# Attention feeding a wide two-layer network on one core: another order list for the first 14 steps

## The chip, the cores and the metric

The kernel runs on one core of one Trainium2 chip. Its time is the device time of one execution in microseconds (us). Five engines work side by side, each through its own instruction queue in order: PE (TensorE, matmuls and transposes), ACT (ScalarE, exponentials, logarithms, copies), DVE (VectorE, reductions and elementwise work), POOL (GpSimd, elementwise work and some transfers) and SP (SyncE, which issues nearly all transfers). An instruction starts when it is at the head of its queue and the results and buffers that it needs are there.

## The reference

```python
# attention: B, H, S, D = 4, 8, 768, 64, block 32, window 16
k_sum = k.reshape(B, H, nb, block, D).max(axis=3)
v_sum = v.reshape(B, H, nb, block, D).mean(axis=3)
scores_l = scale * q @ k.T         # kept where |i - j| < window, else -1e9
scores_s = scale * einsum('bhsd,bhnd->bhsn', q, k_sum) + log(block)
a = softmax(concat([scores_l, scores_s]))     # sum + 1e-9 below
x = (a @ concat([v, v_sum])).transpose(0, 2, 1, 3).reshape(B * S, H * D)
# network: x 3072x512, w_in 512x2048, w_out 2048x512, weights in float64
h = x @ w_in
g = (a[0] + a[1]*h + a[2]*h**2 + a[3]*h**3) / (1 + abs(b[0])*abs(h) + abs(b[1])*h**2 + 1e-6)
out = g @ w_out
```

## The kernel before

The 3072 rows of x are worked in 6 groups of 512, and the 2048 hidden columns in 16 chunks of 128, so that there are 96 steps of one group and one chunk. A step has three parts. The first layer makes h (128x512, in one of two PSUM buffers) with 12 matmuls. The rational function ("gelu" in the code) takes 5 DVE operations and a final one on POOL, with squares, logarithm and exponential on ACT; it writes gh and gl, a high and a low part. The second layer adds 12 matmuls into four accumulators po (po0 to po3). Each factor is split into a high and a low part (xh and xl, gh and gl, two halves of a weight) and three of the four products are summed, which is why a step has 24 matmuls of 512 columns.

The weights come as float64, 1 MB a chunk. They are decoded on the chip: after the load (wr), a scaling on ACT, a byte step on POOL, a shift-and-or on DVE (`SCALAR_TENSOR_TENSOR wr<-wr`), a rounding to the high part (CAST on ACT, or a POOL transfer) and the low part on DVE. The first group needs all 16 chunks decoded.

Attention is made in 48 "halves" of 64 queries (all 8 heads). A half goes through scores (sc, PE), the masked score and its row minimum (4 DVE reductions), exponentials (4 on ACT, then the row sum sm), reciprocal and scaling, transposes (pt, PE), their copy (pts), the product with the values (av, PE), and the parts xh (a cast on ACT or DVE) and xl (a subtraction on DVE). Halves 0 to 7 make the first group's x. The value means that every half of the first batch needs come from window averages on PE (tile vf), copied by ACT into the last 24 rows of vw0 and vw1: before these copies no av matmul can start. The first h matmul needs xh of all 8 halves.

Two PSUM pools matter below: ps_h has two buffers, shared by h, the early pt and the spare matmuls; ps_a has two for the later sc, av and a few squares. So h of step n waits until the buffer of the tile two places earlier in ps_h is free, which for h is when DVE's second-to-last use of it is over (`tu<-tu,cs,h`).

What sets the order in the first 14 steps (NSTRICT = 14) is the table TEXT (line 48), a list of 583 tokens that a loop hands to `token()` one by one; the class Kept records that the instructions of an engine stay in the order in which they were handed out. A token issues the next stage of one thing: `h3` the next stage of half 3, `w4` the next step of decoding chunk 4, `W4` its load, `x5` the next third of the first layer of step 5, `ga5` to `gk5` parts of its rational function, `y5` the next quarter of its second layer, `v2` one term of the value averages, `V2` the load of a window of values, `K`/`k` a load and block maximum of keys, and `Z0` to `Z5` a spare matmul (128x312) whose result is not used. Since each engine has its own queue, a token moved past tokens of other engines alone changes nothing. After the list, the rest of the steps is scheduled by priorities that the change does not touch.

Of the kernel before, what the change touches and what calls it, by code (L numbers as in the profile page):

```python
# [44 lines left out]
LAG = 3  # L45
SOFF = 12
NWARM = 6
TEXT = ("h10 Q0 S0 K0 k0 K2 k2 K1 k1 K3 B9 k3 h8 B8 h2 h3 M0 N0 h3 h3 h3 W0 w0 h2 V2 Q1 h0 h1 h1 h2 N1 h2 V1 h3 h3 V4 V0 W1 W3 Z0 v2 Z4 h0 h0 w0 w0 h4 h2 h1 h1 h1 h4 h0 h0 v4 h2 w0 F0 "
# [11 lines left out]
AVGH = 40  # L60
NCONST = NK + P + AVGH + NB
NREST = (S - HPG * HQ) // P
# [23 lines left out]
def tile_kernel(ctx, tc, qfirst, qw_in, kraw, kwin, vpad, vred, wio, a, b, cboth, out):  # L86
# [660 lines left out]
    strict |= {pe, dve, act, gps, syn}  # L747
    for what in TEXT.split():
        token(what.rstrip("0123456789"), int(what.lstrip("abcdefghijklmnopqrstuvwxyzABCDEFGHIJKLMNOPQRSTUVWXYZ")))
# [100 lines left out]
```

## Time and profile before

| what | value |
|---|---|
| time, median of 3 runs | 629.33 us (628.99 to 630.05) |
| the profiled execution, its own time | 629.38 us |
| its span (first to last instruction) | 627.6 us |
| PE busy | 616.0 us (98%) |
| DVE busy | 563.1 us (90%) |
| ACT busy | 455.4 us (73%) |
| POOL busy | 262.5 us (42%) |
| mean granted clock of PE | 0.996 of full speed |

Busy time of an engine is a mean over stages with different limits: the profile of the first 165 us differs from the rest, so that a row that names a stretch tells more than the whole. A time in brackets behind an instruction, as `[1.78 <-ACT vw L114]`, is how long its engine was idle before it and what ended the wait. All compute instructions carry the line L114 (the helper of Kept), so tiles are told by their names.

### The profile page before, as it was taken

The page shows a single profiled execution, that of the slowest core. Times are in us where ns is not written, and L with a number is a line of the kernel's source. Part 1 is how long each engine was busy: PE and PEld are TensorE (multiplying, and loading weights), DVE is VectorE, ACT ScalarE, POOL GpSimd, SP SyncE. Part 2 cuts the span into 40 slices and gives each one's busy share as a digit, 9 for nine tenths or more (in the row PEclk, how much of TensorE's full clock was granted, in tenths as well). Part 3 has the DMA queues.
Part 4 walks back from the last instruction along what each step waited for, and adds up shares of the span by engine and source line. Part 5 has one row for each costly group of instructions (what it writes and reads, how often), then busy time and mean ns, then how long its engine had stood idle before and what let it go on. Part 6 is the DMA issues. An engine that isn't in the chain of part 4 may idle for free.

```text
span 627.6 us, 11968 instructions
## 1 busy us (share of the span) xinstructions
PE 616.0 (98%) x4126; PEld 491.4 (78%) x4126; DVE 563.1 (90%) x1148; ACT 455.4 (73%) x1022; POOL 262.5 (42%) x359
## 2 busy tenths in 40 slices
PE   8789999999999999999999999999999999999997
PEld 4376777778788888888888888888888888888885
DVE  6989999999798999799999999888888988889885
ACT  3979998986966766867767867757767765755563
POOL 2768747735433435323433245334143242132221
PEclk9989999999999999999999999999999999999999
DMA  8989869332443453333433524224233120100001
GB/s 337 390 296 315 250 178 280 126 116 68 151 131 126 119 159 122 135 99 125 125 106 123 162 83 130 71 66 134 87 113 122 38 66 1 67 1 0 2 1 67
DMA packets 50836, 79.80 MB, mean 127 GB/s; under 512 B 6248, under 2 KB 32040, under 8 KB 48856
## 3 DMA queue, kind: packets, MB, share of 16 engines
q1 hardware_dynamic: 49064, 74.52, 35.7%
q0 software_dynamic: 1280, 4.39, 3.1%
q8 instruction: 32, 0.52, 0.4%
q14 instruction: 28, 0.23, 0.1%
q10 hardware_dynamic: 432, 0.13, 0.1%
HBM read 59.83 MB, written 14.75 MB: 119 GB/s over the span
## 4 chain that ended last, share of the span: by engine, by line
PE 84%; ACT 6%; DVE 4%; POOL 2%; issue 2%; DMA 1%; DVEq 0%; ACTq 0%; POOLq 0%
PE po L114 39%; PE h L114 37%; PE av L114 3%; ACT ss L114 3%; PE sc L114 3%; PE pt L114 1%; DVE tu L114 1%; POOL ss L114 1%; DVE tq L114 1%; DMA cs<-in_b_dram 1%; ACT wearly L114 1%; POOL gl L114 1%; ACT ta L114 1%; DVE gh L114 1%; ACT wr L114 1%
## 5 line engine op out<-in xcount | busy, mean ns | idle before, releaser
L114 POOL TENSOR_TENSOR gl<-tu,ta 128x512 fp32r<-128x512 f32 x96 | 131.2, 1366 | 281.7 <-DVE tu L114 153.7
L114 ACT ACTIVATE ta<-tq,cs 128x512 f32<-128x512 f32 x96 | 69.6, 725 | 72.9 <-DVE tq L114 72.1
L114 PE MATMUL po<-wearly,gh 128*128 128x512 f32 x384 | 120.2, 394 | 0.0
L114 PE MATMUL po<-w,gh 128*128 128x512 f32 x384 | 119.9, 394 | 0.0
L114 POOL TENSOR_SCALAR ss<-ss,sm 128x120 f32<-128x120 f32 x176 | 85.3, 505 | 40.4 <-DVE sm L114 39.6
L114 PE MATMUL h<-xh,wearly 128*128 128x512 f32 x384 | 96.9, 391 | 0.1
L114 PE MATMUL h<-xh,w 128*128 128x512 f32 x384 | 96.5, 390 | 0.0
L114 PEld LDWEIGHTS h<-xh,wearly 128*128 128x128 f32 x384 | 71.5, 188 | 16.4 <-PE spare L114 1.1
L114 PEld LDWEIGHTS po<-wearly,gh 128*128 128x128 f32 x384 | 70.8, 188 | 16.6 <-issue 1.8
L114 PEld LDWEIGHTS h<-xh,w 128*128 128x128 f32 x384 | 71.8, 188 | 15.0
L114 PEld LDWEIGHTS po<-w,gh 128*128 128x128 f32 x384 | 71.1, 188 | 15.7 <-issue 1.3
L114 DVE SCALAR_TENSOR_TENSOR gh<-tu,cs,ta 128x512 fp32r<-128x512 f32 x96 | 74.6, 777 | 8.3 <-ACT ta L114 1.5
L114 ACT ACTIVATE ss<-ss,sm 128x120 f32<-128x120 f32 x188 | 71.8, 386 | 12.7 <-DVE sm L114 12.6
L114 PE MATMUL po<-wearly,gl 128*128 128x512 f32 x192 | 75.1, 391 | 0.3 <-POOL gl L114 0.2
L114 ACT ACTIVATE tu<-h,cs 128x512 f32<-128x512 f32 x96 | 74.8, 779 | 0.4 <-PE h L114 0.4
L114 PE MATMUL po<-w,gl 128*128 128x512 f32 x192 | 74.9, 390 | 0.0
L114 DVE SCALAR_TENSOR_TENSOR tu<-tu,cs,tq 128x512 f32<-128x512 f32 x96 | 72.3, 753 | 2.9
L114 DVE SCALAR_TENSOR_TENSOR tu<-tu,cs,h 128x512 f32<-128x512 f32 x96 | 71.3, 743 | 2.8
L114 DVE SCALAR_TENSOR_TENSOR tq<-tq,gh 128x512 f32<-128x512 f32 x96 | 67.4, 703 | 2.8
L114 ACT ACTIVATE ta<-h,cs 128x512 f32<-128x512 f32 x95 | 64.7, 681 | 3.5 <-POOL gl L114 3.5
L114 DVE TENSOR_TENSOR tu<-tu,h 128x512 f32<-128x512 f32 x96 | 64.9, 676 | 0.0
L114 ACT ACTIVATE ta<-ta 128x512 f32<-128x512 f32 x96 | 60.8, 633 | 2.5
(97 smaller groups left out, 903.3 us busy)
## 6 DMA issues: line engine op xcount, KB each, us to landing
wr<-in_wio_dram SPq DMA_DIRECT2D x15, 1024.0 KB
cross<-tb SPq DMA_DIRECT2D x32, 256.0 KB, 2.0
vw<-in_vpad_dram SPq DMA_DIRECT2D x40, 192.0 KB, 3.4
kw<-in_kwin_dram SPq DMA_DIRECT2D x36, 192.0 KB, 3.3
pts<-cross SPq DMA_DIRECT2D x96, 64.0 KB, 1.9
out_dram<-o SPq DMA_DIRECT2D x23, 256.0 KB, 2.0
qw<-in_qw_dram SPq DMA_DIRECT2D x40, 128.0 KB, 2.6
kr<-in_kraw_dram SPq DMA_DIRECT2D x12, 384.0 KB, 4.5
```

Source lines behind the costliest of these rows:

```text
L114: out = getattr(self.engine, name)(*args, **kw)
```

## The change

Only TEXT changes. It has the same 583 tokens in another order; nothing else in the file differs, so every engine executes the same work. The first two rows of the list of before and of after:

```diff
-TEXT = ("h10 Q0 S0 K0 k0 K2 k2 K1 k1 K3 B9 k3 h8 B8 h2 h3 M0 N0 h3 h3 h3 W0 w0 h2 V2 Q1 h0 h1 h1 h2 N1 h2 V1 h3 h3 V4 V0 W1 W3 Z0 v2 Z4 h0 h0 w0 w0 h4 h2 h1 h1 h1 h4 h0 h0 v4 h2 w0 F0 "
-        "w0 w0 h3 h3 h4 h4 h4 h1 w1 h2 h2 h6 h7 h7 h7 h7 V5 h0 h0 h0 h5 V6 v1 v0 h6 h7 h6 h5 w1 w1 h4 v8 V3 w3 w3 h5 v9 h5 h5 h7 V7 w3 v5 w1 w1 v6 h5 I0 i0 h6 w3 w3 A8 v3 w3 v7 m0 h0 "
...
+TEXT = ("K2 K0 Q0 k0 S0 h10 h11 k2 K1 k1 K3 k3 M0 h8 h2 h2 h0 W0 Z1 h3 h3 Z4 Q1 h6 h1 h1 V0 N0 h2 h2 h2 h2 N1 V1 V2 h3 h3 B8 w0 B9 w0 h0 h0 h0 h3 h3 Z3 h1 h1 h3 h7 h7 h7 w0 h9 v2 W1 "
+        "h0 h4 h3 v1 h5 h7 h1 h6 h0 V4 v4 h4 w1 w1 h6 w1 h0 W3 h0 v0 h1 V7 w0 w0 h5 h5 h4 h4 h7 w1 w1 V6 Z5 v7 w1 w3 w3 w3 v6 V3 v3 h4 h4 h7 F0 v8 v9 V5 v5 h5 h5 I0 i0 w3 A9 A8 h2 w3 "
...
```

The loads of chunks 1 and 3 (tokens `W1`, `W3`) stood together at places 38 and 39 of the list; they stand at 57 and 75 now. In SP's queue, which is all that a load's place among the tokens decides, the 13th and 14th transfers were those of W1 and W3; now the 12th is W1 and the 14th W3, with one window of values between them, and two key loads stand ahead of the first queries.

On ACT the exponentials of the halves are taken in another order. The rows around the copies of the value means (vw0, vw1) were these; ss6 and sm6 are the exponentials and the sum of half 6, wr the scaling of a chunk, pts5 the copied transposes of half 5:

```order
L114 ACTIVATE ss6_418,sm6_419<-ss6_418,sm6_419 128x120 x4
L114 ACTIVATE sm6_419<-sm6_419 128x4
L114 CAST wearly_103<-wr3_259 128x1024
L114 COPY vw0_101<-vf_263 24x512
L114 COPY vw1_102<-vf_263 24x512
L114 CAST xh0_478<-av0_480 128x4x64
L114 ACTIVATE wr4_530<-wr4_530 128x1024
L114 COPY pts5_565<-pt5_551 120x512
L114 ACTIVATE wr2_538<-wr2_538 128x1024
L114 CAST xh0_478<-av4_574 128x4x64
L114 CAST xh0_478<-av3_586 128x4x64
L114 ACTIVATE ss8_524,sm8_525<-ss8_524,sm8_525 128x120 x4
```

and now they are these:

```order
L114 ACTIVATE ss5_412,sm5_413<-ss5_412,sm5_413 128x120 x4
L114 ACTIVATE sm5_413<-sm5_413 128x4
L114 CAST wearly_103<-wr3_400 128x1024
L114 COPY vw0_101<-vf_324 24x512
L114 COPY vw1_102<-vf_324 24x512
L114 CAST xh0_475<-av0_477 128x4x64
L114 ACTIVATE ss6_374,sm6_375<-ss6_374,sm6_375 128x120 x4
L114 ACTIVATE sm6_375<-sm6_375 128x4
L114 ACTIVATE wr2_494<-wr2_494 128x1024
L114 COPY pts5_543<-pt5_530 120x512
L114 CAST xh0_475<-av3_552 128x4x64
L114 ACTIVATE ss8_537,sm8_538<-ss8_537,sm8_538 128x120 x4
```

The exponentials of half 6 stood ahead of the two copies and stand behind the first xh now; those of half 8 come behind the second xh and those of half 9, not in these rows, still ahead of the last xh.

On PE the first steps of the network stood as follows; h0_1 is h of group 0, step 1, vf1 the averages of the second batch, po0_0 the first accumulator of group 0 and spare3 the token Z3:

```order
L114 MATMUL spare3_728<-both_95 128x312
L114 MATMUL h0_1_730<-xh0_478,wearly_103 128x512 x4
L114 MATMUL h0_1_730<-xl0_479,wearly_103 128x512 x4
L114 MATMUL h0_1_730<-xh0_478,wearly_103 128x512 x4
L114 MATMUL vf1_759<-vf1_0_755,both_95 32x128 x4
L114 MATMUL h0_2_796<-xh0_478,wearly_103 128x512 x4
L114 MATMUL h0_2_796<-xl0_479,wearly_103 128x512 x4
L114 MATMUL h0_2_796<-xh0_478,wearly_103 128x512 x4
L114 MATMUL vf1_759<-vf1_1_757,both_95 32x128 x4
L114 MATMUL po0_0_828<-wearly_103,gh0_0_688 128x512 x2
```

and now, from the same h0_1 on:

```order
L114 MATMUL h0_1_747<-xh0_475,wearly_103 128x512 x4
L114 MATMUL pt9_755<-both_95,ss9_546 120x128 x4
L114 MATMUL h0_1_747<-xl0_476,wearly_103 128x512 x4
L114 MATMUL h0_1_747<-xh0_475,wearly_103 128x512 x4
L114 MATMUL h0_2_787<-xh0_475,wearly_103 128x512 x4
L114 MATMUL h0_2_787<-xl0_476,wearly_103 128x512 x4
L114 MATMUL h0_2_787<-xh0_475,wearly_103 128x512 x4
L114 MATMUL pt8_811<-both_95 128x312
L114 MATMUL pt8_811<-both_95,ss8_537 120x128 x4
L114 MATMUL vf1_819<-vf1_0_734,both_95 32x128 x12
L114 MATMUL vf1_819<-vf1_1_736,both_95 32x128 x4
L114 MATMUL h0_3_869<-xh0_475,wearly_103 128x512 x4
```

The spare matmul ahead of h0_1 is gone (all six spares stand ahead of step 0 now, where three of them did before), the transposes of half 9 stand inside h0_1, and h0_3 follows h0_2 without the second layer of step 0 (po0_0 and on) between them. On DVE the rational function of step 1 is finished ahead of that of step 2, where the two were the other way round.

## Rows read from the trace of the kernel before

**Rows 1.** Windows: busy time and count of each engine, PE clock, DMA share, GB/s.
```profile
core 0: us, PE busy (x) PEld busy (x) DVE busy (x) ACT busy (x) POOL busy (x), PEclk, DMA share, GB/s
25.00:32.00 7.00, 5.21 (x32) 1.97 (x30) 6.52 (x9) 6.61 (x22) 5.22 (x5) 1.00 0.93 355
32.00:36.00 4.00, 4.00 (x48) 3.22 (x48) 2.96 (x19) 0.87 (x2) 3.10 (x7) 0.57 1.03 406
36.00:42.60 6.60, 5.02 (x118) 4.29 (x118) 6.06 (x15) 6.08 (x18) 5.41 (x9) 1.00 0.72 241
42.60:92.00 49.40, 49.23 (x361) 36.83 (x360) 48.38 (x99) 48.54 (x106) 32.87 (x35) 1.00 0.82 253
92.00:165.00 73.00, 72.78 (x484) 57.91 (x483) 71.12 (x143) 61.58 (x132) 41.80 (x48) 1.00 0.49 151
```
**Rows 2.** Waits of DVE up to 43 us: us in total, times, longest us.
```profile
DVE ss L114 <- PE sc L114: 1.0, 1, 1.0
DVE xh L114 <- PE av L114: 0.4, 1, 0.4
...
DVE sm L114 <- ACT ss L114: 0.2, 1, 0.2
```
**Rows 3.** Timeline of ACT, 24 to 43 us: start us, us, instruction, [idle before].
```profile
24.36 0.38 ACT L114 ACTIVATE ss<-ss,sm 128x120 f32<-128x120 f32 x1
...
26.11 1.15 ACT L114 CAST wearly<-wr 128x1024 fp32r<-128x1024 f32 x1
...
30.05 1.06 ACT L114 COPY vw<-vf 24x512 f32<-24x512 f32 x2
...
35.98 0.59 ACT L114 COPY pts<-pt 120x512 f32<-120x512 f32 x1 [3.13 <-PE pt L114]
36.47 1.16 ACT L114 ACTIVATE wr<-wr 128x1024 f32<-128x1024 f32 x1
...
41.94 0.67 ACT L114 CAST xh<-av 128x256 fp32r<-128x256 f32 x2
```
**Rows 4.** Timeline of PE, 30 to 64 us.
```profile
30.68 0.69 PE L114 MATMUL av<-pts,vw 120*64 120x64 f32 x16 [1.78 <-ACT vw L114]
...
32.45 1.88 PE L114 MATMUL sc<-kw,qw 64*64 64x120 f32 x32
...
42.66 2.09 PE L114 MATMUL h<-xh,wearly 128*128 128x512 f32 x8
44.59 1.07 PE L114 MATMUL h<-xl,wearly 128*128 128x512 f32 x4
45.59 1.05 PE L114 MATMUL sc<-kw,qw 64*64 64x120 f32 x32
46.57 0.79 PE L114 MATMUL spare<-both 128*128 128x312 f32 x2
47.42 1.20 PE L114 MATMUL h<-xh,wearly 128*128 128x512 f32 x4
...
58.17 1.19 PE L114 MATMUL h<-xh,wearly 128*128 128x512 f32 x4
...
60.08 0.69 PE L114 MATMUL av<-pts,vw 120*64 120x64 f32 x16
...
63.71 1.19 PE L114 MATMUL h<-xh,wearly 128*128 128x512 f32 x4
```
**Rows 5.** Timeline of DVE, 42 to 64 us.
```profile
42.69 0.74 DVE L114 TENSOR_TENSOR xl<-av,xh 128x256 fp32r<-128x256 f32 x2
...
53.19 0.28 DVE L114 CUSTOM_DVE_ANT_0 ss<-sc,both 128x120 f32<-128x120 f32 x1
...
54.00 0.75 DVE L114 SCALAR_TENSOR_TENSOR tq<-sq,cs,ta 128x512 f32<-128x512 f32 x1
54.66 1.22 DVE L114 SCALAR_TENSOR_TENSOR wr<-wr 128x1024 int32<-128x1024 int32 x1
...
57.28 0.75 DVE L114 SCALAR_TENSOR_TENSOR tu<-tu,cs,h 128x512 f32<-128x512 f32 x1
...
62.83 0.73 DVE L114 SCALAR_TENSOR_TENSOR tu<-tu,cs,h 128x512 f32<-128x512 f32 x1
```

20 rows, old and new, of the table TEXT are left out of this document.

## The prediction

> **What bounds the kernel now.** I read the windows first, then the waits of DVE, then the timelines of ACT, PE and DVE over the first 65 us. The windows [rows 1] split the kernel. From 42.6 to 165 us, PE is busy for 49.23 of 49.40 us and then 72.78 of 73.00: there is no idle time on it to remove, and only work taken out, or an earlier start, shortens that stretch. DVE is nearly as full there, 48.38 of 49.40 and 71.12 of 73.00, so that PE cannot run far ahead of DVE: it would catch up with the buffers that DVE still reads. Before 42.6 us no engine is full. PE has 1.79 us idle in 25 to 32 and 1.58 us in 36 to 42.6, and in 32 to 36 its mean granted clock is 0.57 of full speed, so mostly the lower of its two levels, 1.2 GHz.
>
> What the first h matmul (at 42.66 [rows 4]) waits for is a chain over ACT. ACT works without a pause up to the copies of the value means at 30.05 [rows 3]; PE stands idle for 1.78 us until the first av matmul, which those copies release [rows 4]. Then the roles turn: ACT waits 3.13 us for transposes from PE before it copies pts5 [rows 3], since PE first does a block of scores that takes 1.88 us there and 1.05 us at 45.59, at full clock [rows 4]. The last xh casts at 41.94 [rows 3] let h start. DVE waits for that chain too: five waits before 43 us, the longest 1.0 us for those same scores, the shortest 0.2, add up to 2.2 us [rows 2].
>
> So the start of the network is set by ACT's work up to the two copies, and the stretch behind it by PE and DVE together.
>
> **The change part by part.** The sum is made against the profiled execution, 629.38 us, whose span is 627.6 with 1.8 us around it; it is 0.05 us above the median, so that a forecast against the one holds for the other.
>
> *Exponentials of half 6 behind the copies.* One block of exponentials less stands ahead of the copies. A block with its sum takes from 24.36 to 26.11, so 1.75 us [rows 3]; the number of scalings and casts ahead of the copies is unchanged. ACT had no idle time there, hence the copies move from 30.05 to 28.3, and the first av from 30.68 to 28.9. The block itself lands where ACT stood idle for 3.13 us, so it is covered; between the copies and the last xh ACT has one block more and one scaling less (1.16 [rows 3]), 0.6 us net against that idle time. If the cover goes, because PE's transposes come early, ACT is late by 0.6 us at most.
>
> How much of the 1.75 us reaches h? A second bound lies in DVE. Its last xl of this group ends at 43.43 [rows 5]. The order puts one shift-and-or (1.22 [rows 5]) and two reciprocals ahead of it that were behind it, about 1.4 us; the five waits, 2.2 us, are what it can win. So the last xl can come 0.8 us earlier, at 42.6. That costs nothing as long as h's xh part is not over before it: the xl part began at 44.59 [rows 4], and can begin 2.0 us earlier. The start of h moves ahead by 1.75 us, with 2.0 us as the end that DVE sets. If the scores run at full clock, the 0.83 us between 1.88 and 1.05 comes on top but is cut by that same end. On the other side, if PE's transposes or the scores are late as before, all of the gain may be lost. Of 0 to 2.0 I take 1.75, the row of the block.
>
> *Spare matmuls.* Three of the six stand behind the start of h before, none after. The one at 46.57 holds PE until 47.42, 0.85 us [rows 4], in a full stretch. The two others are bounded by 0 (PE waits there for DVE anyway) and 0.85 each; I count them at 0, as PE cannot go on without DVE. Taken ahead of h, each costs PE idle time alone.
>
> *Step 0's second layer behind h_3, and step 1's function ahead of step 2's.* Here the change adds waits. h_3 needs the PSUM buffer of h_1, so it waits for the `tu<-tu,cs,h` of step 1; before, it started at 58.17, right behind that of step 2 at 57.28, which ended 58.03 [rows 4, 5]. In DVE's queue the release of h_1 now takes the place that the release of h_2 had, with one block of score reductions (53.19 to 54.00, 0.81) and one `tq` (0.66) fewer ahead of it and one or two reciprocals: 58.03 - 1.5 - 2.2 = 54.3, the last term DVE's removed waits. PE would be there at about 52.5 to 53.3, since h_3 follows h_2 without the po matmuls: a new wait of 1.0 to 1.8 us, with everything of PE queued behind it. h_4 then needs the release of h_2, whose place is that of h_1's before (62.83, ended 63.56 [rows 5]) less one shift-and-or: 63.56 - 1.1 - 2.2 = 60.3. Before, h_4 began at 63.71 [rows 4]; after, it begins at 60.4, but with three matmuls of po (0.75, at the 1.0 us per four of the xl part [rows 4]) and one av (0.69 [rows 4]) not yet done. Like for like that is 63.71 - 60.4 - 1.44 = 1.9 us ahead of before. Behind h_1 the transposes of half 9 wait for its score reductions too, by hand 0.7 to 0.9 us; that wait is one of those through which PE arrives at h_3, and is in the 1.9.
>
> So PE's early start (1.75) and the spare (0.85) make 2.6 us, and about 0.7 of them is given back in waits for DVE by h_4.
>
> *What is left at the end.* From the 14th step on, the order is that of before, and by then DVE has done the same work. PE, when it waits, waits for DVE: its lead cannot be more than what DVE itself won, 2.2 us and some of the waits of 1.0 and 1.9 us that the two windows from 42.6 to 165 leave it [rows 1]. Between PE's 1.9 at h_4 and DVE's 2.2 there is no room for more; new waits of DVE for ACT, whose work up to 92 us is as full (48.54 of 49.40 [rows 1]), take from it. I allow 0.1 to 0.3 for those and take 1.8: 629.38 - 1.8 = 627.6.
>
> *Loads.* All transfers up to the last window of values carry the same bytes, and the DMA share is 0.93 to 1.03 through 25 to 36 us [rows 1], so the last of them comes no earlier or later; the two key loads ahead of the queries only exchange places in a saturated stretch. I cost them at nothing; at worst a chunk's decoding waits for its load.
>
> **A rule against the trace.** The row shows PE at 0.57 clock in 32 to 36, behind a stretch in which it was busy for 5.21 of 7.00 us, with the 1.78 us idle at its end [rows 1, 4], and back at full clock when it had worked 4.00 us of 4.00. The Trainium skill (TensorE: Matmul & The Clock Gate, section "HAM oscillation — how this bites in real kernels") says that waits between short bursts of matmuls bring the clock down again each time; the trace agrees for this one place, and no row shows it twice. It speaks against this change, which adds waits of PE at h_3.
>
> **The rivals.** *No gain (0.17).* The waits eat the lead: PE's lead meets a full DVE, and of the 2.2 us of DVE's waits only those in front of the copies go, or new ones come. For it: DVE's 0.98 share up to 92 us. Against it: the 1.75 us of ACT lie where ACT has no pause, and DVE's longest wait is a consequence of it. If one third of the gain is left, 0.6 us, the time is 628.8.
>
> *The clock falls a second time (0.07).* At the waits inside h_1 and before h_3 PE would be idle for some 2 us in ten. If 4 us of matmuls then ran at the lower level, as in 32 to 36, they would do what takes about half as long at full clock: 2 us lost, 627.6 + 2.0 = 629.6. Against it: the matmuls around these waits keep PE busy in between, and after 42.6 no window is below 1.00 [rows 1]. The Trainium skill's rule above (TensorE: Matmul & The Clock Gate, same section) would have it this way.
>
> *ACT becomes late and DVE starves (0.14, slower).* In the list two blocks of exponentials and a scaling come ahead of step 10's exponential that came behind it: 2 x 1.75 + 1.16 = 4.7 us [rows 3] of ACT work. If ACT wins the 3.13 us that it waits before 43, it is only 1.6 us later there than before, and DVE, which has two operations of about 1.2 us more ahead of that point as well, does not feel it. It decides whether ACT still waits for PE's transposes in 30 to 43: if that wait stays, DVE stands idle for up to 4.7 less those 2.4, so 2.3 us, in a stretch where it is the limit, while the first part wins 0 to 0.7 of its 1.75 us: 629.4 + 2.3 - 0.7 = 631.0.
>
> *More than forecast (0.06).* The clock does not fall, all three spares count (0.85 each) and DVE wins another 1 us of its waits up to 165: 629.4 - 3.6 = 625.8.
>
> *The load of the chunks comes no later.* In SP's queue W1 is the 12th transfer instead of the 13th and W3 stays the 14th, so the loads are not later at all. This would not move the time; it goes with every case.
>
> **How the numbers follow.** About 0.2% of the time, 1.26 us, is what a measurement of this kernel can tell from no change: faster is below 628.07, slower above 630.59. The forecast has 0.56, with its own range from 626.6 to 628.5; 0.04 of it ends above 628.07. Faster: 0.52 + 0.06 = 0.58. Same: 0.04 + 0.17 + 0.07 = 0.28. Slower: 0.14. The range reaches from the case with more gain into the slower one, 625.8 to 630.8, and leaves out most of the slower case and little of the fastest.
>
> **What would show it.** The copies of vw at 28.0 to 28.7, the first h at 40.6 to 41.4, ACT's wait for pts5 below 1.5 us and DVE's waits up to 43 us below 1 us confirm the first step. A wait of PE for DVE of over 0.8 us at h_3 and DVE at or over 0.97 busy from 43 to 157 confirm the second. The forecast is wrong if the copies don't move, if ACT stays idle for 3 us behind them, if the clock is below 1 beyond 43 us, or if DVE waits for ACT by more than 1 us between 60 and 130; and if the time is above 628.5 with all of that in place, the lead was lost behind the 14th step, which I hold for settled by equal orders.

## The result, and the profile after

The changed kernel takes 633.45 us (median of 7 runs, 630.91 to 635.08) against 629.33 us (7 runs, 628.69 to 630.13): the ratio is 1.0054, with an interval of 1.0037 to 1.0072. It is slower by 4.1 us where 1.8 us less was forecast, and its runs spread three times as wide. The profiled execution is the longest of the seven, 635.08 us with a span of 633.1, so that the losses read from it are up to 1.6 us larger than those of the median.

The windows that answer to [rows 1]:

```profile
25.00:32.00 7.00, 6.59 (x66) 3.09 (x65) 6.97 (x12) 6.59 (x24) 6.66 (x8) 1.00 1.05 413
32.00:36.00 4.00, 3.80 (x75) 3.24 (x75) 3.97 (x22) 3.83 (x14) 3.82 (x8) 1.00 0.99 408
36.00:42.60 6.60, 5.86 (x74) 4.16 (x69) 6.60 (x14) 6.47 (x17) 6.21 (x8) 1.00 0.78 241
42.60:92.00 49.40, 41.43 (x295) 31.49 (x296) 43.75 (x86) 40.84 (x81) 33.33 (x33) 0.97 0.87 267
92.00:165.00 73.00, 72.61 (x512) 58.22 (x511) 69.23 (x129) 61.62 (x129) 39.83 (x47) 1.00 0.41 122
```

The column before the DMA share is the mean granted clock of PE. Up to 42.6 us the change does what was forecast: DVE is full (6.97 of 7.00, 3.97, 6.60), ACT nearly so, and the clock stays at full level in 32 to 36. The loss lies between 42.6 and 92: PE is idle for 8.0 us there (0.2 before), ACT for 8.6 (0.9 before), DVE for 5.7 (1.0 before). On the timeline of PE the rows that answer to [rows 4], and the two waits that have no counterpart before:

```profile
28.91 0.69 PE L114 MATMUL av<-pts,vw 120*64 120x64 f32 x16
...
40.26 2.12 PE L114 MATMUL h<-xh,wearly 128*128 128x512 f32 x8
42.56 1.17 PE L114 MATMUL h<-xl,wearly 128*128 128x512 f32 x4 [0.18 <-DVE xl L114]
...
54.27 1.19 PE L114 MATMUL h<-xh,wearly 128*128 128x512 f32 x4 [0.40 <-DVE tu L114]
...
61.39 1.19 PE L114 MATMUL h<-xh,wearly 128*128 128x512 f32 x4 [0.26 <-DVE tu L114]
...
79.75 0.62 PE L114 MATMUL pt<-both,ss 128*120 128x128 f32 x4 [1.76 <-POOL ss L114]
...
85.17 1.08 PE L114 MATMUL pt<-both,ss 128*120 128x128 f32 x4 [2.69 <-DVE tq L114]
```

The first av starts 1.77 us earlier and h 2.40 us. By step 14, from which the order is that of before, the lead has become a delay: h of that step starts at 135.97, and at 131.47 before. The first of the two waits is for POOL, which scales the exponentials of a half (ss) late since it had itself waited for the load of a chunk, issued behind that of chunk 15:

```profile
73.31 1.13 POOL L114 TENSOR_SCALAR wr<-wr 128x1024 int32<-128x1024 uint8 x1 [2.63 <-DMA wr<-in_wio_dram]
```

What stands behind the wait at 85.17 is told by the chain of waits:

```profile
67.62 1.66 POOL gl L114
69.28 0.56 POOL wearly L114
69.83 10.90 DMA w<-wr
...
81.72 0.58 ACT sq L114
82.30 0.60 ACT ta L114
82.90 0.68 ACT tu L114
...
83.67 0.13 DVE tu L114
...
85.17 1.08 PE pt L114 x4
```

A transfer that POOL issues, the rounding of chunk 8 to its high part (`w<-wr`, 512 KB), takes 10.90 us. ACT needs it to make the negative of that part, and since ACT works in order, the squares and the linear term of the next step's function wait behind; DVE waits for those, and PE for DVE. The idle times, on ACT and on DVE:

```profile
67.56 1.06 ACT L114 ACTIVATE wearly<-wearly 128x1024 fp32r<-128x1024 f32 x1 [1.82 <-DMA wearly<-wr]
...
80.76 1.06 ACT L114 ACTIVATE w<-w 128x1024 fp32r<-128x1024 f32 x1 [2.38 <-DMA w<-wr]
```

```profile
83.67 0.69 DVE L114 TENSOR_TENSOR tu<-tu,h 128x512 f32<-128x512 f32 x1 [2.62 <-ACT tu L114]
```

Before, the same transfer was issued later and came sooner. POOL's issue and ACT's use of it in the kernel before, one line from each engine's timeline, then the line of the transfer's group (count, KB, us from issue to landing), which gave 10.9 in the changed kernel:

```profile
76.19 0.62 POOL L114 DMA_DIRECT2D w<-wr  x1
```

```profile
82.72 1.04 ACT L114 ACTIVATE w<-w 128x1024 fp32r<-128x1024 f32 x1
```

```profile
w<-wr POOLq DMA_DIRECT2D x1, 512.0 KB, 2.9
```

It landed 2.9 us after its issue, at 79.1, and ACT came to it 3.6 us later without a wait. In the changed kernel POOL issues it 6.4 us earlier, right behind another transfer of its own:

```profile
69.21 0.90 POOL L114 DMA_DIRECT2D wearly<-wr  x1
69.83 0.85 POOL L114 DMA_DIRECT2D w<-wr  x1
```

and it lands 1.6 us later. The windows of the two kernels around it, before and then after:

```profile
56.00:69.00 13.00, 13.00 (x140) 9.52 (x139) 12.77 (x21) 12.75 (x28) 9.97 (x12) 1.00 0.91 238
69.00:82.00 13.00, 12.94 (x61) 10.20 (x60) 12.52 (x34) 12.68 (x32) 10.88 (x13) 1.00 0.69 248
82.00:92.00 10.00, 10.00 (x71) 7.84 (x70) 9.86 (x14) 9.90 (x16) 3.40 (x3) 1.00 0.68 190
```

```profile
56.00:69.00 13.00, 11.74 (x90) 8.81 (x89) 12.70 (x17) 9.44 (x22) 6.72 (x5) 1.00 0.91 265
69.00:82.00 13.00, 10.12 (x72) 7.69 (x71) 10.39 (x30) 10.52 (x24) 10.19 (x14) 1.00 1.01 312
82.00:92.00 10.00, 7.31 (x29) 5.75 (x28) 8.13 (x11) 9.71 (x22) 5.23 (x5) 0.83 0.54 139
```

The DMA share in 69 to 82 us is 1.01 in place of 0.69. The new order has put the load of chunk 15 (1 MB, two issues of 512 KB) from 102.6 us to 58.1 us and four loads of queries and keys from about 90 us to 75 us, into the stretch in which chunks 9 to 11 are loaded. What fills the engines while the transfer runs is told by the queues, here for 71 to 75 us and then for 75 to 81 (packets, MB, share of the 16 engines); q0 carries the transfers that POOL issues, q1 those of SP:

```profile
q0 software_dynamic: 224, 0.86, 101.2%
q1 hardware_dynamic: 30, 0.08, 4.8%
```

```profile
q1 hardware_dynamic: 725, 1.91, 87.8%
q0 software_dynamic: 53, 0.15, 10.5%
```

So up to 75 us POOL's two transfers of 512 KB fill the engines themselves, and what is left of them comes slowly beside SP's loads, issued at 70.98 us and from 75.13 on. Two things lie in the 10.9 us, then: the transfer ahead in the same queue, and the loads. The Trainium skill (DMA: Bandwidth & Descriptors, section "Issuing engines are not separate DMA queues") says that transfers from SP, ACT and POOL run on the same 16 DMA engines and interleave; the second of these stretches, in which both queues move data, agrees with it.

After the two waits of 1.76 and 2.69 us the clock falls, 0.83 in the mean of 82 to 92 us. That is the rule weighed in the prediction (the Trainium skill, TensorE: Matmul & The Clock Gate, section "HAM oscillation — how this bites in real kernels"), and the trace agrees with it, at another place: a second fall does come, behind the waits for POOL and DVE of 78 to 85 us and not behind those at h_3. The loss does not hang on it: three of the seven executions of the changed kernel have a mean granted clock of 1.000, and they took 630.91, 633.45 and 633.75 us.

### The profile page after: what moved, and what is told of

It is laid out like the page before. It is cut to its first block, busy times and chain, and to the rows that moved or that the text cites. A ratio compares the mean times of both kernels' runs of the same rounds, so it can differ in the third digit from the quotient of the medians.

```text
span 633.1 us, 11982 instructions
## 1 busy us (share of the span) xinstructions
PE 616.8 (97%) x4126; PEld 491.9 (78%) x4126; DVE 564.8 (89%) x1148; ACT 455.7 (72%) x1022; POOL 265.5 (42%) x359
## 4 chain that ended last, share of the span: by engine, by line
PE 80%; DVE 8%; ACT 7%; DMA 3%; issue 2%; POOL 1%; DVEq 0%; ACTq 0%; POOLq 0%; SPq 0%
PE po L114 37%; PE h L114 35%; PE av L114 3%; ACT ss L114 3%; PE sc L114 2%; DMA w<-wr 2%; DVE tq L114 2%; ACT ta L114 2%; DVE tu L114 1%; PE warm L114 1%; DMA wr<-in_wio_dram 1%; ACT wr L114 1%; DVE gh L114 1%; DVE wr L114 1%; DVE ss L114 1%
```

## The experiments

Theory 1 is that the loss comes from transfers: the early load of chunk 15 fills the DMA engines, and ACT stands in order behind POOL's transfers. Theory 2 is that it comes from the order of the first steps' second layer and functions, where the prediction had placed new waits of PE.

The kernels ran in four jobs beside runs of the kernel before, which gave medians of 629.77, 629.95, 629.95 and 629.79 us there (629.33 in the job of the changed kernel); the ratio takes this into account, a difference of two medians of different jobs does not. Some lists take one row more, so that the line of all compute instructions is L115 there.

| kernel | median us | ratio to before, 95% |
|---|---|---|
| changed | 633.45 | 1.0054 (1.0037 to 1.0072) |
| changed, W15 late | 632.11 | 1.0042 (1.0029 to 1.0056) |
| changed, negation of chunk 8 later | 632.25 | 1.0033 (1.0021 to 1.0045) |
| changed, both | 630.54 | 1.0000 (0.9989 to 1.0010) |
| changed, both, second layer ahead of h_3 | 630.56 | 1.0008 (0.9996 to 1.0021) |
| before, W15 early | 633.34 | 1.0052 (1.0039 to 1.0065) |
| before, negation of chunk 8 earlier | 631.35 | 1.0020 (1.0009 to 1.0032) |
| old start, new rest | 636.50 | 1.0094 (1.0080 to 1.0109) |
| new start, old rest | 629.14 | 1.0009 (0.9987 to 1.0031) |
| new start, old rest, W15 later | 628.65 | 0.9982 (0.9970 to 0.9993) |
| before, half 6 behind the copies | 628.33 | 0.9974 (0.9964 to 0.9984) |
| the same, spares ahead of h | 629.96 | 1.0005 (0.9990 to 1.0019) |
| the same, and W15 later | 629.25 | 0.9992 (0.9981 to 1.0002) |

**The early load.** The load of chunk 15 is moved back:

```diff
 w8 w8 h12 w7
-W15
 gd2 gi2 h8 u2
...
 y0 w7 w8 w6
-w15
 x4 h8 ga4 gc4
...
 h12 y6 y6 W13
+W15
...
 h14
+w15
 w15 x12 x12 y8
```

> The changed order with one load moved back: W15 (1 MB) stands behind W13 again, and the scaling of chunk 15 behind it, so that the load leaves some 45 us later. Theory 1 (transfers): the early W15 keeps the DMA engines full from 56 to 80 us, POOL's transfers of the high parts of chunks 7 and 8 land 7 to 11 us after their issue in place of 3 to 5, and ACT, DVE and PE stand behind them in order; without it ACT's two waits for them (1.8 and 2.4 us) fall below 1 us each and the time is 628 to 630. Theory 2 (order of the second layer): the loss comes from po behind h_3 and step 1's function ahead of step 2's, and W15 is no part of it; the time stays at 632 to 634.

The median is 632.11 us, 1.3 lower, which the two intervals don't separate. The wait of ACT for chunk 7 is gone, and so is POOL's for a load (PE then waits 0.30 us for POOL in place of 1.76); but that for chunk 8 is not: the transfer takes 9.39 us by the chain of waits, and ACT stands before it.

```profile
78.53 1.06 ACT L115 ACTIVATE w<-w 128x1024 fp32r<-128x1024 f32 x1 [2.99 <-DMA w<-wr]
```

So W15 is not what makes that transfer long, and theory 1 as it stood holds only in part. POOL still issues it 0.62 us behind its transfer of chunk 7. The mirror of it, W15 early in the order of before:

```diff
 w6 V9 gk2 u5
+W15
 x3 h12 w7 x3
...
 w11 w6
+w15
 w9 gk3 w8 w6
```

> The order of before with that one load early: W15 behind the last term of the second batch's value averages (u5), some 40 us earlier, and its scaling among the steps of chunk 6. Theory 1: POOL's transfers land later in 55 to 85 us and the time grows to 630.5 to 633. Theory 2: no change, 629.0 to 629.8.

This gave 633.34 us, 3.6 more than before, by one load of 1 MB and a scaling. The link is another here: the transfers that SP issues behind W15 are late. PE waits 2.13 us for one of them, a block of keys (kw), then ACT 1.40 us for a load, and DVE 2.10 us for ACT.

```profile
70.36 1.16 PE L115 MATMUL sc<-kw,qw 64*64 64x120 f32 x32 [2.13 <-DMA kw<-ks]
...
77.30 1.15 ACT L115 ACTIVATE wr<-wr 128x1024 f32<-128x1024 f32 x1 [1.40 <-DMA wr<-in_wio_dram]
```

```profile
84.85 0.75 DVE L115 SCALAR_TENSOR_TENSOR tq<-sq,cs,ta 128x512 f32<-128x512 f32 x1 [2.10 <-ACT ta L115]
```

**The early wait.** The last two steps of chunk 8 are moved back:

```diff
 h11 gk3 gj4
-w8
 ga5 gb5 x6 ge5
...
 x7 x7 h12 h10
+w8
 w9 w9 w9 gk5
```

> The changed order with the fifth and sixth step of chunk 8 later: the negation on ACT that waits for the high part stands 23 tokens further back, behind ACT's parts of step 5's function, and the accumulating transfer 19 tokens further back. Theory 1, with ACT's order as the link: the transfers land as late as in the changed kernel but ACT no longer waits for chunk 8 ahead of step 5's function, DVE's wait of 2.6 us goes, and the time is 629.5 to 631.5 unless chunk 8 itself is late for its step. Theory 2: 632 to 634.

The median is 632.25 us, 1.2 lower, which the intervals don't separate either. In its trace, which is of one of its two fastest executions (630.13 us), no wait of ACT for chunk 8 is left, though the transfer takes 9.8 us still; a wait of 1.97 us for chunk 7 is. The mirror in the order of before moves the negation up:

```diff
 w6 w9 gk3 w8
+w8
 w6 h12 gb5 ga5
...
 gd5 gi5 gj5 h13
-w8
 w8 x6 x6 ga6
```

> The order of before with the negation of chunk 8 on ACT earlier, right behind the start of the transfer that it waits for. Theory 1, the link in ACT's order: ACT waits some 2 to 3 us for the transfer, DVE runs out of work behind it, and the time is 630.3 to 632.5. If such a wait is absorbed: 629.3 to 630.0.

It costs 1.4 us (631.35), with a transfer that takes 3.0 us and no load moved. ACT itself waits only 1.00 us for a load and 0.43 for the transfer, not 2 to 3, but with its work of 1.06 us ahead of step 5's function this makes DVE wait:

```profile
77.72 1.17 ACT L114 ACTIVATE wr<-wr 128x1024 f32<-128x1024 f32 x1 [1.00 <-DMA wr<-in_wio_dram]
...
79.32 1.06 ACT L114 ACTIVATE w<-w 128x1024 fp32r<-128x1024 f32 x1 [0.43 <-DMA w<-wr]
```

```profile
82.17 0.75 DVE L114 SCALAR_TENSOR_TENSOR tq<-sq,cs,ta 128x512 f32<-128x512 f32 x1 [2.58 <-ACT ta L114]
```

Both edits in the changed kernel:

> The changed order with both edits, W15 behind W13 and the last two steps of chunk 8 later. Theory 1: the two gains of 1.3 and 1.2 us add, 629.3 to 631.0, and no wait of ACT for a transfer over 1 us is left in 60 to 90 us. If one of the two waits only hides behind the other, 631 to 632.5.

They gave 630.54 us, 2.9 below the changed kernel (3.5 if each is read beside its own runs of before), and the ratio to before is 1.0000. Against the kernels with one edit alone the intervals don't touch: by these comparisons the early W15 costs 1.7 us and the early negation 1.6. ACT comes to chunk 8 without a wait, and DVE is full again in 69 to 82 us:

```profile
82.98 1.07 ACT L114 ACTIVATE w<-w 128x1024 fp32r<-128x1024 f32 x1
```

```profile
69.00:82.00 13.00, 12.70 (x87) 9.74 (x86) 12.93 (x34) 12.17 (x32) 11.33 (x14) 1.00 0.95 285
82.00:92.00 10.00, 9.90 (x70) 7.73 (x69) 9.66 (x13) 9.97 (x17) 5.31 (x4) 1.00 0.67 178
```

**Start and rest.** The list is cut at the first part of step 0, behind 181 tokens of the order of before or 182 of the changed one, and the start of one is joined with the rest of the other. The first of the three:

```diff
-h10 Q0 S0 K0 k0 K2
...
+K2 K0 Q0 k0 S0 h10
...
 x0 x0 w2 w2 x0 w5 w4
```

> The changed order up to the first part of step 0, then all remaining tokens in the order of before. The forecast's first step alone: h starts at 40 to 41 us and the lead of some 2 us is kept up to the end, 627 to 628.3. If the lead is lost to DVE whatever the order behind it, the time is 629.0 to 629.8.

> The order of before up to the first part of step 0, then all remaining tokens in the changed order. Theory 1 (the loss lies behind step 0, where the order asks for chunks 7 and 8 before the transfers deliver them): h starts at 42.5 to 43 us, ACT and DVE wait in 60 to 90 us as in the changed kernel, 632.5 to 635. Theory 3 (the loss comes from how the new start meets what follows, e.g. an earlier start that only moves the waits): 629 to 630.5.

> The new start with the old rest, and W15 later still, behind W14, which takes 1 MB out of the full stretch from 92 to 110 us. Theory 1: the executions of 630 to 635 us that the same kernel without this edit shows become fewer, and the median is 628.0 to 629.0. If that stretch is not what makes them: 629.1 with the same spread.

With the old rest the new start gives 629.14 us, ten of twelve executions between 628.76 and 630.99 and two at 634.8 and 635.5; with W15 later still, 628.65 and none above 629.95. With the old start the new rest gives 636.50, 6.5 more than before. So the loss comes with the rest; the changed kernel, with the new start, loses 4.1 us beside its own runs of before, 2.4 less. This split is not exact, as a join can make waits of its own (shown further down). Twelve executions of each don't show what made the two long ones. The trace of the kernel with the new start and the old rest is of the longest, 635.46 us: PE waits 2.94 us there for a transfer of values that SP had issued 13.2 us before, and the trace with W15 later, of an execution of 629.69 us, has no such wait.

**The forecast's first term alone.**

```diff
 v6 h5 I0 i0
-h6
 w3 w3 A8 v3
...
 v7 m0 h0 h0
+h6
 h0 A9 h4 h4
```

> The order of before with one token moved: the exponentials of half 6 stand behind the copies of the value means and the first xh. The forecast's first term alone: the copies at 28.0 to 28.7 us, h at 40.6 to 41.3, and as the rest is unchanged the time is 627.3 to 628.6. If the lead is lost to waits for DVE or for transfers behind step 0: h as early, and 629.0 to 629.8.

This is the lowest median of all versions, 628.33 us (627.96 to 628.89), 1.6 below the 629.95 of before in the same job. The copies, the wait for pts5 and the start of h by ACT's and PE's timelines:

```profile
28.95 1.06 ACT L114 COPY vw<-vf 24x512 f32<-24x512 f32 x2
...
34.37 0.58 ACT L114 COPY pts<-pt 120x512 f32<-120x512 f32 x1 [0.85 <-PE pt L114]
```

```profile
41.15 2.11 PE L114 MATMUL h<-xh,wearly 128*128 128x512 f32 x8
```

The copies come 1.1 us earlier and h 1.5 us; at step 14 h is 0.7 us ahead (130.76 against 131.47). Not all of the 1.6 us need be ACT's block. The clock of 0.57 in 32 to 36 us, which the trace of before shows, is not in every execution of the old start: the trace of the kernel of before with the negation earlier, whose start is the same, has 1.00 there and starts h at 41.95, so that h is 0.8 us earlier here at a like clock. In this job 15 of the executions of before have a mean granted clock of 0.997 or less and a median of 630.35 us, and 9 have 1.000 and 629.16; all seven of this version have 0.999 or 1.000. Against executions of like clock the edit wins 0.8 us; that the rest comes from the fall, which its seven executions don't show, is argued and not tried.

**The spares.** Three tokens are moved in that kernel, and in a second one W15 as well:

```diff
 w4 w4 h9 Z5
+Z1 Z2 Z3
 w5 w5 x0 x0
...
 h10 h11 h11 gb0
-Z3
...
 h12 h12 y1 y1
-Z2
...
 ga12 gb12 gc12 ge12
-Z1
```

> The order of before with half 6's exponentials behind the copies and, in addition, the three spare matmuls that stood behind h_0 (Z1, Z2, Z3) taken ahead of it. The forecast's second term: 0.85 us less than with the first edit alone, which gave 628.3, so 627.3 to 627.8. If PE only meets DVE sooner, no more than 0.2 us: 628.1 to 628.5.

> The same two edits and W15 behind W14, as in the kernel that took the load out of 92 to 110 us. If transfers still cost something there: 0.3 to 1 us below the version without this edit, with less spread. If not: the same within 0.3 us.

Both missed: 629.96 and 629.25 us. The place was ill chosen, in front of h with PE no longer idle: four spare matmuls take the 2 us up to 42.50, and h starts 1.35 us later than without the edit. From h_0 to h_1 0.75 us of that comes back, as the term said. Then PE meets DVE at h_7, 0.89 us:

```profile
40.51 2.37 PE L114 MATMUL spare<-both 128*128 128x312 f32 x8
42.50 2.20 PE L114 MATMUL h<-xh,wearly 128*128 128x512 f32 x8
...
46.52 1.21 PE L114 MATMUL h<-xh,wearly 128*128 128x512 f32 x4
...
82.13 1.19 PE L114 MATMUL h<-xh,wearly 128*128 128x512 f32 x4 [0.89 <-DVE tu L114]
```

**What is left of the loss.** 630.54 with both edits is still 1.4 to 2.2 us above the versions with the old rest. Its interval lies within that of the new start with the old rest (629.14), overlaps a little with that of the same with W15 later (628.65), and lies clear of that of the one edit in the order of before (628.33).

```diff
 ga2 gc2 u5 gb2
+y0 y0
 x3 A12 x3 ge2 gf2
-y0
 w8 w8 w8 h12
...
 w6 w6 x3 ga3
-y0
 x4 x4 gk1 gj2
```

> The changed order with W15 and chunk 8's negation later (630.5 us) and, in addition, the first two quarters of step 0's second layer ahead of h_3 again. Theory 2 as the rest of the loss: the waits of 0.40 us at h_3 and 0.88 at h_4 are filled, 629.3 to 629.9. If DVE sets the pace there, PE waits as long elsewhere: 630.2 to 630.8.

With the second layer ahead of h_3 again the median is 630.56: theory 2, as far as this edit goes, does not explain the rest. (In the profiled execution h starts at 42.79, and at 40.78 in that of the kernel that this one is made from, with the same order up to there: starts of single profiles differ by up to 2 us, so that a difference of starts read from two profiles is one of single executions.) Two further kernels switch to the old order later, at step 4 and at step 7:

> The changed order with W15 and chunk 8's negation later, up to the first part of step 4; all remaining tokens in the order of before. If what is left of the loss (630.5 against 628.3 to 628.7 with the old rest) lies in the waits of steps 1 to 3, the second layer behind h_3 and the functions of steps 1 and 2 changed round: 630.0 to 630.8. If it lies behind them: 628.3 to 629.2.

> The same, with the changed order up to the first part of step 7 and the order of before from there. If what is left lies between steps 4 and 7: 630 to 630.8 here and under 629.2 with the switch at step 4. If it lies behind step 7: 628.3 to 629.2 in both.

They gave 636.56 us (ratio 1.0124, 1.0089 to 1.0160) and 632.16 us (1.0035, 1.0023 to 1.0046), both above the highest that was expected, and tell nothing of the rest of the loss: the trace of each has a long wait that the kernel with both edits does not have. One line of PE from each:

```profile
70.04 1.22 PE L114 MATMUL po<-wearly,gh 128*128 128x512 f32 x2 [4.49 <-ACT vn L114]
```

```profile
93.60 1.19 PE L114 MATMUL h<-xh,w 128*128 128x512 f32 x4 [2.30 <-DMA w<-wr]
```

## Why the prediction was wrong

- *The copies and the start of h: right.* Copies forecast at 28.3 us, measured 28.28; first av 28.9, measured 28.91; h between 40.6 and 41.4, measured 40.26, with the clock at 1.00 in 32 to 36; ACT's wait of 3.13 us for pts5 is gone, and so are the five waits of DVE. One reading was off and did no harm: between the copies and the last xh ACT has three blocks of exponentials (halves 6, 8 and 9) where it had one, so two more and not one, and the wait of 3.13 us covers these too. The bound by DVE was right too: the last xl was put at 42.6, and the xl part starts at 42.56 after a wait of 0.18 for it. That something of the term reaches the end is shown by the kernel with this edit alone: 1.6 us, 0.8 against executions of like clock.
- *The spares: right in size, not shown at the end.* 0.75 us came back between h_0 and h_1 where 0.85 was counted, in a kernel whose spares then stood in the way of h.
- *h_3 and h_4: right place, a smaller wait.* The release of h_1 was put at 54.3 and h_3 started at 54.27, but PE waited 0.40 us, not 1.0 to 1.8, because PE came there at 53.9 and not at 52.5 to 53.3 (the wait for half 9 inside h_1 was 0.74 us, as counted). h_4 came at 61.39 where 60.4 was forecast, so 0.9 us ahead of before like for like and not 1.9; PE had waited 1.00 us more for ACT's copy of the transposes of half 8. Moving the second layer back gained nothing.
- *"What is left at the end", with "Loads": the step that failed.* It held a lead at h_4 for a lead at step 14, because DVE's and PE's work in between was the same, and it cost the loads at nothing after looking only at those up to 36 us. In place of the 1.8 us ahead that it took, h of step 14 came 4.5 us late. The order from step 4 on was not read: W15 moved from 102.6 to 58.1 us, POOL's transfer of chunk 8 fell right behind that of chunk 7 and beside the loads and landed 10.9 us after its issue, and ACT's negation stood ahead of step 5's function. Together the early load and the early negation are 2.9 us, the difference that both edits make. The sentence "at worst a chunk's decoding waits for its load" named the mechanism and gave it no price. The signs of being wrong that the prediction had named came: DVE waited 2.62 us for ACT at 83.67, the clock fell beyond 43 us, and DVE was busy for 105.0 of the 114 us from 43 to 157 (0.92), not 0.97.
- *The slower rival: right sign, wrong cause, and 2.4 us short.* DVE did starve behind ACT, and 631.0 was given for it, 633.45 measured; but ACT was late because of a transfer in its order, not for the exponentials of step 10, and its wait for pts5, which the rival needs, had gone. That its sign was right is luck.
- *The clock.* A second fall came in the profiled execution, at 84 to 88 us (0.59), behind the waits of PE of 78 to 85 us; the executions of 633.45 and 633.75 us show a mean clock of 1.000, so it is not the loss.
- *The new order's loads of chunks 1 and 3*, which were said not to matter, were not tried by themselves; the start as a whole is not shown to gain with the old rest (1.0009, 0.9987 to 1.0031), and gains a little with W15 later as well (0.9982, 0.9970 to 0.9993).
- *Open.* Why the changed order with both edits does not keep the lead of its start: at a ratio of 1.0000 it shows nothing of the 1.8 us that were forecast. In its trace PE waits in seven places between 46 and 108 us for DVE or ACT, 0.28 to 0.88 us each; no kernel here takes these away without adding others. The trace of the new start with the old rest and W15 later does not keep it either: h starts at 40.42, 2.2 us ahead of before, and at step 14 at 131.59, 0.1 us behind it, after a wait of PE for DVE at h_3:

```profile
58.42 1.20 PE L114 MATMUL h<-xh,wearly 128*128 128x512 f32 x4 [2.12 <-DVE tu L114]
```

  How much of POOL's 10.9 us is due to its own transfer of chunk 7 and how much to the loads is open too: no kernel here puts the two transfers apart and leaves the rest.

## What to carry to other kernels

When an order list changes, read every queue of it to the end, not only the place where the profile says that the kernel waits: 2.9 us were lost some 40 us behind the start of h, which the change had brought forward, through one load that had moved 45 us ahead and one operation on ACT that came too early. An operation that waits for a transfer, on an engine that works in order, is as late as the transfer and makes all behind it late; its distance in the list should be read against what the DMA engines carry in that stretch, the same engine's other transfers among it, and not against the transfer's time alone (2.9 us here where it was alone, 10.9 behind another and beside loads). A clock that falls in one profile need not fall in every execution, so a gain read from that profile should be held against executions of like clock. And a start can be taken over without the rest: one token of this change, the exponentials of half 6, was worth 1.6 us alone, 0.8 of them at a like clock.

## What the runs showed of the hardware

- The same POOL transfer of 512 KB between buffers on the chip, the high part of chunk 8, took 2.9 to 3.9 us where POOL had issued no other just before (nine kernels), and 8.2 to 10.9 us where it was issued 0.6 us behind another of 512 KB, with loads from SP before its end (seven kernels). In the changed kernel, issued 6.4 us earlier, it landed 1.6 us later. With none of POOL's ahead of it but beside loads, the transfer of 512 KB that POOL issues at 93.03 us in the kernel before took 9.0 us, at a DMA share of 0.96 from 93 to 102 us.
- Executions of one order differ in the granted clock: the two kernels with the old start whose traces show 0.57 and 1.00 in 32 to 36 us have the same instructions up to there.
- The executions of the version with one edit lie between 627.96 and 628.89 us, those of the changed kernel between 630.91 and 635.08, with the same instructions. What widens the spread is not shown: the kernel with both edits, without the long waits, spreads from 628.71 to 631.25.
